# Attention, a dense MoE and a top-2 MoE in one kernel: the first expert's rows chosen in f32r, gate logits in 32-column tiles, bias rows of the start given to other engines, and named banks in the attention

## The chip, the cores and the metric

The kernel runs on one core of a Trainium2 chip. The time is the device time of one launch in microseconds (us); lower is better. A core has four compute engines with a queue each, which work in order: TensorE (PE; its weight loads are listed as PEld), VectorE (DVE), ScalarE (ACT) and GpSimd (POOL). SyncE (SP) issues most DMAs. Engines wait for one another by semaphores.

## The reference

Three stages follow one another, all in float32.

```python
scores = scale * q @ k.T                      # B=2, H=8, S=576, D=64
x = log1p(|i-j|) / log1p(max(i,1))
bias = relu(x * w1 + b1) @ w2                 # hidden 32, one bias per head
attn = softmax(scores + bias);  x = attn @ v  # -> 1152 tokens x 512
g = max(0.01*h, h), h = x @ w_in              # first MoE: 512 -> 2048 -> 512, dense
x = g @ w_out
noisy = x @ w_gate + log1p(exp(x @ w_noise)) * noise   # second MoE: 8 experts
top2, softmax over the two
out[mask] += weight * relu(x[mask] @ w1[e]) @ w2[e]    # 512 -> 1024 -> 512
```

## The kernel before, in words

**Attention.** Tokens go in nine blocks of 128 queries; a block has four pairs of heads, so there are 36 pairs. A pair's scores are made by TensorE (L1138), VectorE adds the bias and takes the row minimum (`add_bias`, L1149, tile `s`), ScalarE exponentiates (L1162), TensorE transposes the probabilities in three steps (`tp`, L1181 and L1183), each into a PSUM bank named `m` which ScalarE copies out (`tp_copy`, L1189, tile `pts`), and TensorE multiplies by V (`pv`, L1206). The banks named `m` are a pool of four under one name; the pool hands them out.

**The bias** is built in 36 groups of 16 queries; the first query block needs groups 0 to 7. A group is four `bias_relu` rows of 128x576 (on GpSimd for groups from `POOLED` = 5 on, L1034; otherwise three on VectorE, L1038, and one on ScalarE, L1036), eight matmuls with column tiles of 32 (`bias_mm`, L1048), a copy `bt` (ScalarE L1058 or L1060, VectorE L1062), and a store that rearranges it into the tile `bias` (L1069). Groups on GpSimd use a table of negated offsets. `add_bias` of the first pair needs the stores of groups 0 to 7.

**First MoE.** Weights and activations are split into a high and a low float32r part (`whi`, `wlo`, `xah`, `xal`), and each product is three float32r matmuls (L312 up, L342 to L344 down). Tokens go in two groups, five tiles of 128 and then four.

**Gate.** Each finished tile of 128 tokens is transposed (`gate_trans`, L363), copied out (`xt`, L370, L372) and multiplied by the 16 gate and noise columns (`gate_logits`, L380, four float32 matmuls with the 128 tokens as weights and 16 moving columns). A group's chain then follows: `gate_softplus` on ScalarE (tile `ez`, two functions with a table load each), `gate_top2` on VectorE, `gate_count` on TensorE (L431 to L434), `gate_slots`. Tiles are gated in the groups 0 to 2, 3 and 4, 5 and 6, 7 and 8.

**The passage.** Tokens are scattered by expert to `xs` in memory. For the first expert that is too late for tiles 5 to 8: their rows are chosen by a matmul with a 0/1 selection matrix (`sel` on VectorE, L517; `x_sel` on TensorE, L523, 128x320 in float32), and the rows of tiles 0 to 4 come back from memory and are added by matmuls with the identity (`x_early`, L528). The sums are split into `xah` and `xal` (L543, L545), and the first expert's `e_mm1` (also L312) and `e_mm2` (L584) follow.

**Order.** A planner of this kernel, `Plan`, is given every step with its engine, an estimated duration, the resources read and written, and a due time, and fixes the order of each engine's queue. Where a matmul in float32 is one row of the program, the trace shows two instructions.

Of the kernel before, what the change touches and what calls it, by code (L numbers as in the profile page):

```python
# [18 lines left out]
P = 128  # L19
# [11 lines left out]

BLOCKS = [(b, t) for t in range(4) for b in range(2)] + [(None, 4)]
# [9 lines left out]
POOLED = 5  # L42
# [89 lines left out]
class Moe:  # L132
# [15 lines left out]
    def steps(self, ident, zrow):  # L148
# [27 lines left out]
        def loads():  # L176
            self.wg = cp.tile([P, DC, 2 * E], F32, name="wg")
            nc.sync.dma_start(self.wg, self.t["wg"])
            self.nz = cp.tile([P, NT, E], F32, name="nz")
            nc.sync.dma_start(self.nz, self.t["nz"])  # L180
# [173 lines left out]

    def store_x2(self, t):
        for p0, m, t0 in token_runs(t):
            self.nc.sync.dma_start(self.x2d[t0:t0 + m, :], self.rows[t][p0:p0 + m, 0, :DM])
# [7 lines left out]
    def gate_copy(self, t, eng, c=slice(0, DM)):  # L365
        if ("xt", t) not in self.T:
            self.T["xt", t] = self.wk.tile([P, DC, P], F32, name="xt")
# [6 lines left out]
    def gate_logits(self, t, i, bank):  # L374
# [3 lines left out]
        lp = self.R["lp"][:, i * 2 * E:(i + 1) * 2 * E]  # L378
        for d in range(DC):
            self.nc.tensor.matmul(lp, xt[:, d, :], self.wg[:, d, :], start=(d == 0), stop=(d == DC - 1))  # L380

    def gate_softplus(self, nb, step):
        if step == 0:
            self.R["lg"] = lg = self.R["lp"][:, :nb * 2 * E].rearrange("p (i e) -> p i e", i=nb)
# [99 lines left out]
    def load_x(self, e, t):  # L484
        o, n = STILES[t]
        self.XR[e, t] = r = self.row()
        if e != "early":
            o, n = o + e * C1, P
# [8 lines left out]
    def load_early(self, q):  # L497
        self.load_x("early", q)
# [6 lines left out]
    def sel(self, t, i):  # L505
# [5 lines left out]
        self.T["sel", t] = s = self.T["sels"].pop(0).bitcast(F32)  # L511
# [126 lines left out]
    def run(self):  # L638
# [6 lines left out]
        def weight(n, key):  # L645
# [17 lines left out]
            wait = [("sel", NT - 3)] if n == U1 else [("x", 0, DC - 1)] if U1 < n < U1 + 8 else []  # L663
            add("ACT", .95, self.split, (n, 0), [f] + wait, [w], key - 4)
            add("DVE", 1.15, self.split, (n, 1), [f, w] + [("first", 0)] * (n == 1), [w], key - 4)
            return w

        def gates(ts, key):

            t0, nb = ts[0], len(ts)  # L670
            early = [("xe", q) for q in range(3)] if t0 >= GROUPS[1][0] else []
            for q, tt in enumerate(ts):
# [3 lines left out]
                xt = slot("xt", 2)  # L676
                new = [xt, ("xt1", xt[1])]
                add("PE", .43, self.gate_trans, (tt, 2 if late else 0), [row[tt, 0], row[tt, 3]], [b] + new, k)
# [3 lines left out]
                else:  # L682
                    add("ACT", .27, self.gate_copy, (tt, "ACT", half[0]), [b], new[:1], k)
                    add("DVE", .33, self.gate_copy, (tt, "DVE", half[1]), [b], new[1:], k)
                add("PE", .86, self.gate_logits, (tt, q, 1), new, [("tp", 1)], k + 45 * late)
# [16 lines left out]
            for q, tt in enumerate(ts):  # L702
                if tt >= GROUPS[1][0]:
                    first = tt == GROUPS[1][0]
                    if first:
                        sels[0] = slot("g", 5)
                    add("DVE", .3, self.sel, (tt, q), [("rec", 0), ("iota", 0)] + [sels[0]] * (not first),
                        [("sel", tt)] + [sels[0]] * first, k + 20 * (tt < NT - 2) - .2)
# [14 lines left out]

        def evac(i, tt, key):
# [9 lines left out]
            if tt < NT - 2:  # L734
                add("DVE", .6, self.evac_x2, (tt, i, 1, "DVE"), [(f"acc{i}", 0)] if tt < GROUPS[1][0] else [row[tt, 0], row[tt, 3]],
                    [row[tt, 1]], key + .2 + 60 * (tt >= b0 > 0))
# [19 lines left out]
        def up(g, f, k):  # L756
# [3 lines left out]
            xk = [("xb", d) for d in range(DC)] if g else []  # L760
# [13 lines left out]
        def x_sel(tt, d, key):  # L774
            add("PE", .54, self.x_sel, (tt, d), [("sel", tt), sels[0], row[tt, 0], row[tt, 3]], [(f"acc{d}", 0)], key)

        for g, (b0, nb, n) in enumerate(GROUPS):
            chunks = range(nb * P // n)
            tail = 4 if g else 0
            for f in range(nf1 - tail):  # L780
# [7 lines left out]
                if g == 0 and f in (10, 11, 12, 13):  # L788
                    d = f - 10
                    add("ACT", .53, self.split_x, (d, 0), [], [("xb", d)], t + 8)  # L790
                    add("DVE", .61, self.split_x, (d, 1), [("xb", d)], [("xb", d)], t + 8)
# [26 lines left out]
        for d in range(DC):  # L818
            for tt in (NT - 4, NT - 3):
                x_sel(tt, d, t + 10 + tt)  # L820

            add("PE", .27, self.x_early, (d,), [("xe", q) for q in range(3)] + [("tp", 0)], [(f"acc{d}", 0)], t + 20)
            for tt in (NT - 2, NT - 1):
                x_sel(tt, d, t + 30 + d + .1 * tt)
# [40 lines left out]
        for e in range(E):  # L865
            for f in range(nf2):
# [3 lines left out]
                h, gf = slot("h", 2), slot("g", 5)  # L870
                for part in [[d] for d in range(DC)] if e + f == 0 else [range(DC)]:
# [9 lines left out]
                if f == 0 and e == 0:  # L881
                    load(1, t)
                    add("DVE", .1, self.overflow_flag, (0,), [("rec", 0)], [("m", 0)], t)
                    b = ("tp", 0)
                    add("PE", .1, self.overflow_flag, (1,), [("m", 0)], [b], t)
                    add("DVE", .1, self.overflow_flag, (2,), [b], [], t)
# [85 lines left out]
class Attn:  # L972
    def __init__(self, ctx, tc, t, xa, xb, ident):
# [10 lines left out]
        self.ps_m = ctx.enter_context(tc.tile_pool(name="ps_m", bufs=4, space=bass.MemoryType.PSUM))  # L984
# [10 lines left out]
        nc.vector.tensor_scalar(self.scb[:, n:], self.scb[:, n:], small[:, 1:2], -1.0, op0=OP.mult, op1=OP.mult)  # L995
# [471 lines left out]
```

## Time and profile before

| | us |
|---|---|
| time, median of 3 runs (lowest to highest) | 685.68 (684.35 to 686.38) |
| time of the profiled execution | 689.21 |
| its span | 687.5 |
| TensorE busy in it | 654.7 |

The span runs from the first to the last recorded instruction; the profiled execution lasted 1.7 us longer than its span and 3.5 us longer than the median. Rows of the trace are given below, ahead of the prediction. In a timeline row the first number is the start, the second the length of the merged stretch, `x3` the number of instructions, and the bracket the idle time ahead of it and what ended it.

### The profile page before, as it was taken

Reading aid. Unit: us, or ns where it says so; the run is one execution under the profiler, and the core shown is the slowest. Engines: PE = TensorE matmul, PEld = TensorE weight load, DVE = VectorE, ACT = ScalarE, POOL = GpSimd, SP = SyncE. Lnnn points to the kernel's source line nnn. Section 1 sums busy time; section 2 is a strip of 40 time slices with the busy share of each in tenths; the row PEclk is TensorE's granted clock in tenths of the full one; section 3 lists DMA queues with packets and bytes.
Section 4 is the critical chain, followed back from the end, with each engine's and each line's share of the span. In section 5 each row is a group of like instructions: output and inputs, shape, how many; then the busy total and the mean of one; then the engine's idle time right before and its main releaser. Section 6 shows DMA issues by size and latency. Waiting matters only on the chain.

```text
span 687.5 us, 14783 instructions
## 1 busy us (share of the span) xinstructions
PE 654.7 (95%) x5777; PEld 553.0 (80%) x5777; DVE 458.0 (67%) x1010; ACT 342.9 (50%) x657; POOL 180.9 (26%) x215
## 2 busy tenths in 40 slices
PE   6799999999999998999999999999999999999992
PEld 2467766777789987999988997898888889888881
DVE  7589887976879878946656435565656465565621
ACT  5367766676674333445545345544434444444420
POOL 6867655541000000000042003103133140403311
PEclk9889999999999999999999999999999999999997
DMA  3785862326356787735245404658585776858521
GB/s 115 200 231 167 272 208 69 91 54 212 110 185 184 224 242 240 247 89 184 77 155 157 128 31 139 214 185 257 173 247 172 239 215 198 273 174 270 167 66 40
DMA packets 41629, 118.60 MB, mean 173 GB/s; under 512 B 6100, under 2 KB 6356, under 8 KB 39506
## 3 DMA queue, kind: packets, MB, share of 16 engines
q1 hardware_dynamic: 36850, 105.47, 49.8%
q0 software_dynamic: 4560, 11.71, 5.1%
q8 instruction: 47, 0.77, 0.5%
q10 hardware_dynamic: 144, 0.41, 0.2%
q14 instruction: 28, 0.23, 0.1%
HBM read 77.91 MB, written 30.75 MB: 158 GB/s over the span
## 4 chain that ended last, share of the span: by engine, by line
PE 79%; DVE 9%; DMA 5%; ACT 3%; issue 2%; POOL 0%; DVEq 0%; ACTq 0%; POOLq 0%
PE h L312 28%; PE acc L584 17%; PE m L1206 5%; PE sc L1138 5%; PE m L1181 4%; PE m L1048 4%; PE acc L344 4%; PE acc L342 3%; PE acc L343 3%; DMA wr<-in_w_in 3%; ACT pts L1189 2%; PE acc L523 1%; DMA wr<-in_w_out 1%; PE acc L380 1%; PE sc L1048 1%
## 5 line engine op out<-in xcount | busy, mean ns | idle before, releaser
L286 DVE TENSOR_TENSOR wlo<-wr,whi 128x1024 fp32r<-128x1024 f32 x96 | 117.1, 1222 | 55.9 <-ACT whi L283 51.4
L312 PE MATMUL h<-xah,whi 128*128 128x320 f32 x384 | 120.5, 314 | 0.3 <-DVE gg L329 0.3
L283 ACT ACTIVATE whi<-wr 128x1024 fp32r<-128x1024 f32 x96 | 101.2, 1056 | 36.4 <-PE acc L584 13.3
L312 PE MATMUL h<-xal,whi 128*128 128x320 f32 x384 | 119.1, 310 | 0.1
L312 PE MATMUL h<-xah,wlo 128*128 128x320 f32 x384 | 118.6, 309 | 0.0
L1034 POOL TENSOR_SCALAR up<-wl,small 128x576 f32<-128x576 f32 x124 | 96.9, 798 | 55.8 <-PE m L1048 46.0
L584 PE MATMUL acc<-whi,g 128*128 128x512 f32 x320 | 106.7, 398 | 0.0
L618 POOL DMA_INDIRECT out<-row x24 | 35.4, 1475 | 178.9 <-DVE row L609 140.2
L312 PEld LDWEIGHTS h<-xah,whi 128*128 128x128 f32 x384 | 72.4, 189 | 7.9 <-DVE gg L329 1.4
L558 ACT ACTIVATE g<-h 128x320 fp32r<-128x320 f32 x64 | 28.0, 437 | 98.8 <-PE h L312 43.9
L473 POOL DMA_INDIRECT xs<-rows,sidx x18 | 20.2, 1120 | 213.0 <-ACT lk L326 145.0
L312 PEld LDWEIGHTS h<-xal,whi 128*128 128x128 f32 x384 | 72.4, 189 | 4.5 <-DVE xal L545 0.9
L584 PE MATMUL acc<-wlo,g 128*128 128x512 f32 (+1 forms) x192 | 75.7, 395 | 0.0
L312 PEld LDWEIGHTS h<-xah,wlo 128*128 128x128 f32 x384 | 72.3, 188 | 0.0
L565 DVE SCALAR_TENSOR_TENSOR g<-h,g 128x64 fp32r<-128x64 f32 (+1 forms) x128 | 35.4, 318 | 51.9 <-ACT g L558 50.9
L1189 ACT ACTIVATE pts<-m 128x384 f32<-128x384 f32 (+1 forms) x108 | 50.0, 523 | 38.7 <-PE m L1181 35.2
L584 PEld LDWEIGHTS acc<-whi,g 128*128 128x128 f32 x320 | 56.9, 188 | 8.7
L344 PE MATMUL acc<-whi,g 128*128 128x512 f32 x144 | 56.8, 394 | 2.4 <-DVE g L333 2.4
L342 PE MATMUL acc<-whi,g 128*128 128x512 f32 x144 | 57.5, 399 | 0.0
L1162 ACT ACTIVATE pp<-s,mn 128x576 f32<-128x576 f32 x72 | 54.9, 767 | 5.1 <-DVE mn L1149 5.1
L343 PE MATMUL acc<-wlo,g 128*128 128x512 f32 x144 | 57.1, 396 | 0.0
L1149 DVE CUSTOM_DVE_ANT_0 s<-sc,bias 128x576 f32<-128x576 f32 x72 | 51.4, 747 | 1.1 <-PE sc L1138 1.1
(160 smaller groups left out, 1212.4 us busy)
## 6 DMA issues: line engine op xcount, KB each, us to landing
wr<-in_w SPq DMA_DIRECT2D x64, 512.0 KB
bias<-bt SPq DMA_DIRECT2D x40, 288.0 KB
wr<-in_w_in SPq DMA_DIRECT2D x8, 1024.0 KB
wr<-in_w_out SPq DMA_DIRECT2D x8, 1024.0 KB
wf<-wr SPq DMA_DIRECT2D x16, 512.0 KB
wr<-wf SPq DMA_DIRECT2D x16, 512.0 KB
row<-xs SPq DMA_DIRECT2D x23, 258.0 KB
xs<-xb SPq DMA_DIRECT2D x4, 1290.0 KB
```

The lines of the kernel that those rows point to most:

```text
L283: self.nc.scalar.activation(w[0], r, AF.Copy)
L286: self.nc.vector.tensor_tensor(out=lo, in0=r, in1=hi.bitcast(F32), op=OP.subtract)
L312: self.nc.tensor.matmul(h, u[:, d, :], v[:, d, :], start=(d == 0 and i == 0), stop=(d == DC - 1 and i == 2))
L342: nc.tensor.matmul(acc, gh, whi, start=(f == 0), stop=False)
L343: nc.tensor.matmul(acc, gh, wlo, start=False, stop=False)
L344: nc.tensor.matmul(acc, gl, whi, start=False, stop=(f == self.FF1 // P - 1))
L565: self.nc.vector.scalar_tensor_tensor(gl, h[:, c], 0.0, g[:, c].bitcast(F32), op0=OP.max, op1=OP.subtract)
L584: nc.tensor.matmul(y, u, v, start=(f == 0 and i == 0), stop=(last and i == len(prods) - 1))
L1034: self.nc.gpsimd.tensor_scalar(u, w, 3.0e38, b, op0=OP.min, op1=OP.max)
L1149: self.nc.vector.tensor_tensor_reduce(out=s.rearrange("p (a b) -> p a b", a=2), in0=sc[:, :, :288], in1=bias[:, h, :].rearrange("p (a b) - ...
L1162: self.nc.scalar.activation(p[:, a * SEQ:(a + 1) * SEQ], s, AF.Exp, bias=mn[:, 0:1], scale=-1.0, accum_out=sm[:, 0, a:a + 1])
L1189: self.nc.scalar.activation(ps, self.PT[blk, c, k][:, :n, :], AF.Copy)
```

## The change

It has four parts. **At the start** `POOLED` goes from 5 to 8: the 12 bias rows of groups 5, 6 and 7 leave GpSimd, nine for VectorE and three for ScalarE; the groups are built in the order 0 to 7; and the negated table with the part of `wl` that only GpSimd reads is prepared by a new step `negate` behind VectorE's last row, for which GpSimd's first row now waits. **In the attention** the four banks `m` get names of their own, `m0` to `m3`, and are used in turn. **At the gate** the logits of tiles 0 to 6 are made by `gate_quads`: the 16 gate columns, padded to 32, are the weights, a tile's 128 tokens are the moving columns, and each tile of a group has a column tile of 32 of its own; the result is copied and transposed back. Tiles 7 and 8 keep `gate_logits`. **In the passage** each of the rows of tiles 5 to 8 is split into a high and a low float32r part (`split_row`), `sel` is written as float32r, and `x_sel` is two float32r matmuls instead of one in float32. `x_early` always takes 128 rows. The copies of tiles 5 and 6, their `sel` and the overflow flag are held back to later places, the pieces of the first `e_mm1` come behind all of `x_sel`, and the first weight of the second MoE is split earlier.

```diff
-POOLED = 5
+POOLED = 8
+EARLY = [0, 128, C1 - 128]
...
+    def gate_quads(self, ts, bank):
+        xt = [self.T.pop(("xt", t)) for t in ts]
+        self.R["lq"] = lq = self.bank(bank)
+        for d in range(DC):
+            for i, x in enumerate(xt):
+                self.nc.tensor.matmul(lq[32 * i:32 * i + 32, :P], self.wg[:, d, :], x[:, d, :],
+                                      start=(d == 0), stop=(d == DC - 1))
+    def gate_quads_copy(self, nb):
+        self.nc.vector.tensor_copy(self.lt[:32 * nb, :], self.R["lq"][:32 * nb, :P])
+    def gate_quads_trans(self):
+        self.R["lp"] = lp = self.R["lq"][:, P:2 * P]
+        self.nc.tensor.transpose(lp, self.lt, self.ident)
...
+    def split_row(self, t, step):
+        hi, lo = self.row_parts(t)
+        r = self.rows[t][:, 0, :DM].rearrange("p (d c) -> p d c", d=DC)
+        if step == 0:
+            self.nc.scalar.activation(hi, r, AF.Copy)
+        else:
+            self.nc.vector.tensor_tensor(out=lo, in0=r, in1=hi.bitcast(F32), op=OP.subtract)
...
-        self.nc.tensor.matmul(self.T["x", 0, d][:, :C1], self.rows[t][:, 0, d * P:(d + 1) * P], self.T["sel", t],
-                              start=first, stop=(t == NT - 1))
+        for i, x in enumerate(self.row_parts(t)):
+            self.nc.tensor.matmul(self.T["x", 0, d][:, :C1], x[:, d, :], self.T["sel", t],
+                                  start=(first and i == 0), stop=(t == NT - 1 and i == 1))
...
-            self.nc.tensor.matmul(self.T["x", 0, d][:, o:o + n], self.XR["early", q][:n, d * P:(d + 1) * P],
-                                  self.ident[:n, :n], start=False, stop=False)
+            self.nc.tensor.matmul(self.T["x", 0, d][:, o:o + n], self.XR["early", q][:, d * P:(d + 1) * P],
+                                  self.ident[:, P - n:], start=False, stop=False)
...
-            wait = [("sel", NT - 3)] if n == U1 else [("x", 0, DC - 1)] if U1 < n < U1 + 8 else []
+            wait = [("we", 0)] if n == U1 + 1 else [("x", 0, DC - 1)] if U1 + 1 < n < U1 + 8 else []
...
+    def bank(self):
+        self.banks += 1
+        return self.ps_m.tile([P, 512], F32, name=f"m{self.banks % 4}")
...
+    def negate(self):
+        n = 4 * POOLED
+        self.nc.vector.tensor_scalar(self.scb[:, n:], self.scb[:, n:], self.small[:, 1:2], -1.0, op0=OP.mult, op1=OP.mult)
+        self.scale_wl(slice(WL1, WL1 + P))
...
-        for i, G in enumerate((0, 5, 1, 2, 6, 3, 4, 7)):
+        for i, G in enumerate(range(8)):
...
+        add("DVE", .5, self.negate, (), [("row6.2", 0)], [("neg", 0)], -2.2)
```

VectorE's queue at the start, before (`pp` and `u` are bias rows, `ql` and `kp` splits of Q and K, `bt` the copies of groups 8 and 9, the last row `add_bias`):

```order
L1006 TENSOR_SCALAR wl<-wl,small 128x807
L1038 TENSOR_SCALAR pp<-wl,small 128x576 x3
L1038 TENSOR_SCALAR u<-wl,small 128x576 x3
L1109 SCALAR_TENSOR_TENSOR ql<-raw,qh 128x512
L1038 TENSOR_SCALAR pp<-wl,small 128x576 x3
L1083 TENSOR_TENSOR kp_97<-raw,kp_97 128x576
L1038 TENSOR_SCALAR u<-wl,small 128x576 x3
L1038 TENSOR_SCALAR pp<-wl,small 128x576 x3
L1062 TENSOR_SCALAR bt<-m,small 128x288 x2
```

The same place of the change:

```order
L1117 TENSOR_SCALAR pp<-wl,small 128x576 x3
L1117 TENSOR_SCALAR u<-wl,small 128x576 x3
L1188 SCALAR_TENSOR_TENSOR ql<-raw,qh 128x512
L1117 TENSOR_SCALAR pp<-wl,small 128x576 x3
L1117 TENSOR_SCALAR u<-wl,small 128x576 x3
L1162 TENSOR_TENSOR kp_96<-raw,kp_96 128x576
L1117 TENSOR_SCALAR pp<-wl,small 128x576 x3
L1117 TENSOR_SCALAR u<-wl,small 128x576 x3
L1117 TENSOR_SCALAR pp<-wl,small 128x576 x3
L1117 TENSOR_SCALAR u<-wl,small 128x576 x3
L1088 TENSOR_SCALAR small<-small 128x112
L1079 TENSOR_SCALAR wl<-wl,small 128x128
```

VectorE has 24 bias rows there instead of 15, and the last two rows, `negate`, are what GpSimd's first row waits for.

TensorE's queue in the passage, before, behind the logits of tile 7 (`h` is the bank of tile 8's transposes, the four `acc` the four quarters of the model width):

```order
L363 MATMUL h<-ident,rows 128x128 x4
L523 MATMUL acc_6028<-g,rows 128x320
L523 MATMUL acc_6036<-g,rows 128x320
L380 MATMUL acc_6006<-wg,xt 128x16 x4
L523 MATMUL acc_6048<-g,rows 128x320
L523 MATMUL acc_6054<-g,rows 128x320
```

The same place of the change, from tile 8's transposes on:

```order
L380 MATMUL h<-ident,rows 128x128 x4
L397 MATMUL acc_6011<-wg,xt 128x16 x4
L557 MATMUL acc_6056<-g,xbh 128x320
L557 MATMUL acc_6056<-g,xbl 128x320
L557 MATMUL acc_6061<-g,xbh 128x320
L557 MATMUL acc_6061<-g,xbl 128x320
```

No `x_sel` stands between the transposes and the logits of tile 8 any more; 16 float32r rows of tiles 5 and 6 follow them, then half of `x_early`, the count (L464 to L467), and the rest.

Further on in the same queue, before, behind `x_early` (`xah` and `xal` are the first expert's input, `ofm` the overflow flag):

```order
L523 MATMUL acc_6028<-g,rows 128x320 x2
L633 MATMUL tp<-ident,ofm 1x128
L523 MATMUL acc_6036<-g,rows 128x320 x2
L312 MATMUL h<-xah,whi 128x320
L312 MATMUL h<-xal,whi 128x320
L312 MATMUL h<-xah,wlo 128x320
L523 MATMUL acc_6048<-g,rows 128x320
```

The same place of the change, the end of `x_sel` and the beginning of the first expert:

```order
L557 MATMUL acc_6070<-g,xbh 128x320
L557 MATMUL acc_6070<-g,xbl 128x320
L557 MATMUL acc_6070<-g,xbh 128x320
L557 MATMUL acc_6070<-g,xbl 128x320
L317 MATMUL h<-xah,whi 128x320
L317 MATMUL h<-xal,whi 128x320
L317 MATMUL h<-xah,wlo 128x320
```

The first expert's pieces no longer stand between the selections; the 16 float32r rows of tiles 7 and 8 are all ahead of them, and the flag is behind.

## Rows read from the trace of the kernel before

**Rows 1.** The page: span; busy time, share, instructions of each engine

```profile
span 687.5 us, 14783 instructions
PE 654.7 (95%) x5777; PEld 553.0 (80%) x5777; DVE 458.0 (67%) x1010; ACT 342.9 (50%) x657; POOL 180.9 (26%) x215
```

**Rows 2.** Windows: stretch, busy us (instructions), PEclk, DMA share, GB/s

```profile
404.00:438.00 34.00, 33.67 (x203) 27.47 (x203) 18.62 (x91) 18.38 (x36) 7.87 (x8) 1.00 0.33 110
438.00:660.00 222.00, 222.00 (x1267) 197.64 (x1266) 136.73 (x237) 100.69 (x156) 56.11 (x42) 1.00 0.70 217
...
29.18:31.50 2.32, 2.22 (x12) 1.71 (x12) 1.24 (x5) 1.51 (x4) 2.32 (x4) 0.50 0.82 209
```

**Rows 3.** Line L1038: ns least/median/most, first and last start

```profile
L1038 DVE TENSOR_SCALAR pp<-wl,small x9: 520/995/1002, 6.1 to 19.5; 128x576 f32<-128x576 f32 x9
```

**Rows 4.** Timeline of VectorE and GpSimd, 5 to 33 us: start, length

```profile
8.34 2.83 DVE L1038 TENSOR_SCALAR u<-wl,small 128x576 f32<-128x576 f32 x3
14.36 0.74 DVE L1083 TENSOR_TENSOR kp<-raw,kp 128x576 fp32r<-128x576 f32 x1
...
6.14 15.72 POOL L1034 TENSOR_SCALAR up<-wl,small 128x576 f32<-128x576 f32 x16 [4.76 <-DVE wl L1006]
22.44 2.90 POOL L1034 TENSOR_SCALAR up<-wl,small 128x576 f32<-128x576 f32 x4 [0.58 <-PE sc L1048]
```

**Rows 5.** Timeline of ScalarE at the start

```profile
6.42 0.76 ACT L1036 ACTIVATE pp<-wl,small 128x576 f32<-128x576 f32 x1
7.08 0.67 ACT L1081 ACTIVATE kp<-raw 128x576 fp32r<-128x576 f32 x1
13.33 0.74 ACT L1058 ACTIVATE bt<-sc,small 128x576 f32<-128x576 f32 x1
```

**Rows 6.** The chain that ended last, 20 to 29 us, in order of time

```profile
22.84 0.84 ACT bt L1060
23.70 3.65 DMA bias<-bt
28.36 0.66 DVE s L1149
```

**Rows 7.** Timeline of TensorE before the first transposes

```profile
29.18 1.50 PE L1138 MATMUL sc<-kp,qh 64*128 64x288 f32 x4 [2.32 <-DVE mn L1149]
31.56 1.75 PE L1181 MATMUL m<-ident,pp 128*128 128x128 f32 x7
```

**Rows 8.** Waits of TensorE, 95 to 115 us, and its timeline there

```profile
PE m L1181 <- ACT pts L1189: 2.6, 4, 0.6
...
101.09 0.55 PE L1181 MATMUL m<-ident,pp 128*128 128x128 f32 x3 [0.64 <-ACT pts L1189]
102.66 0.27 PE L1183 MATMUL m<-ident,inv 128*128 128x128 f32 x1
102.86 1.18 PE L1048 MATMUL m<-up,small 128*32 128x288 f32 x16
103.86 1.06 PE L1206 MATMUL m<-pts,vt 128*32 128x128 f32 x32
```

**Rows 9.** Timeline of TensorE at the gate of the first tiles

```profile
333.50 0.96 PE L380 MATMUL acc<-wg,xt 128*128 128x16 f32 x8
```

**Rows 10.** Timeline of TensorE in the passage

```profile
420.91 3.48 PE L523 MATMUL acc<-g,rows 128*128 128x320 f32 x12
424.49 4.06 PE L528 MATMUL acc<-ident,row 128*128 128x128 f32 x24
437.30 0.31 PE L312 MATMUL h<-xah,wlo 128*128 128x320 f32 x1
437.45 0.63 PE L584 MATMUL acc<-whi,g 128*128 128x512 f32 x2
```

**Rows 11.** Timeline of ScalarE and VectorE at the last tiles' gate

```profile
421.09 0.18 ACT L386 ACTIVATE ez<-acc 128x16 f32<-128x16 f32 x1 [1.16 <-issue]
...
425.93 0.68 DVE L517 TENSOR_SCALAR g<-iota_c,y 128x320 f32<-128x320 f32 x2
```

More of the change, by code (lines that the diff above doesn't have):

```diff
@@ L683, in gates @@
                     add("ACT", .27, self.gate_copy, (tt, "ACT", half[0]), [b], new[:1], k)
-                    add("DVE", .33, self.gate_copy, (tt, "DVE", half[1]), [b], new[1:], k)
-                add("PE", .86, self.gate_logits, (tt, q, 1), new, [("tp", 1)], k + 45 * late)
+                    add("DVE", .33, self.gate_copy, (tt, "DVE", half[1]), [b], new[1:] + [("turned", 0)], k)
+                if late:
+                    add("PE", .86, self.gate_logits, (tt, q, 1), new, [("tp", 1)], k + 45)
+            if not late:
+                add("PE", .6, self.gate_quads, (ts, 1), sum(xts, []), [("tp", 1)], k)
+                add("DVE", .25, self.gate_quads_copy, (nb,), [("tp", 1)], [("lt", 0)], k)
+                add("PE", .2, self.gate_quads_trans, (), [("lt", 0)], [("tp", 1)], k)
+            for x in later:
+                x(key + 60, [("turned" if late else "lt", 0)])
+            later.clear()
+            if late:
+                for q, tt in enumerate((NT - 4, NT - 3)):
+                    add_sel(tt, q, key + 50, [("turned", 0)])
             k = key + .5
@@ L701, in gates @@
             add("DVE", 1.6, self.gate_slots, (t0, nb), [R, ("ef", 0), ("we", 0), ("tp", 0)], [("rec", 0)], k)
[L702 to L708, printed above, removed]
+            if late:
+                for q, tt in enumerate(ts):
+                    add_sel(tt, q, k - .2, [])
             for q, tt in enumerate(ts):
@@ L722, in gates, with copies @@
                 add("DVE", .08 * nb, self.gate_run, (nb,), [R], [("run", 0)], k + .3)
+        def copies(i, tt, key, wait):
+            r, x = [row[tt, 0], row[tt, 3]], [(f"xb{d}.{i // 2}", 0) for d in range(DC)]
+            add("ACT", .53, self.split_row, (tt, 0), r + wait, x + [("rh", tt)], key + .1)
+            add("DVE", .6, self.split_row, (tt, 1), r + [("rh", tt)] + wait, [("rl", tt)], key + .1)
+            if tt < NT - 2:
+                add("DVE", .6, self.evac_x2, (tt, i, 1, "DVE"), r + wait, [row[tt, 1]], key)
         def evac(i, tt, key):
@@ L774, in x_sel @@
         def x_sel(tt, d, key):
-            add("PE", .54, self.x_sel, (tt, d), [("sel", tt), sels[0], row[tt, 0], row[tt, 3]], [(f"acc{d}", 0)], key)
+            add("PE", .29, self.x_sel, (tt, d), [("sel", tt), sels[0], ("rh", tt), ("rl", tt)], [(f"acc{d}", 0)], key)
         for g, (b0, nb, n) in enumerate(GROUPS):
@@ L819, in run @@
             for tt in (NT - 4, NT - 3):
-                x_sel(tt, d, t + 10 + tt)
-            add("PE", .27, self.x_early, (d,), [("xe", q) for q in range(3)] + [("tp", 0)], [(f"acc{d}", 0)], t + 20)
+                x_sel(tt, d, t + 6 + .1 * tt)
+            add("PE", .6, self.x_early, (d,), [("xe", q) for q in range(3)], [(f"acc{d}", 0)], t + 7.5)
             for tt in (NT - 2, NT - 1):
-                x_sel(tt, d, t + 30 + d + .1 * tt)
+                x_sel(tt, d, t + 7 + .3 * d + .1 * tt)
         xsall = [("xs", tt, x) for tt in range(NT) for x in range(2)]
@@ L1044, in bias_mm @@
         else:
-            bp = self.ps_m.tile([P, 512], F32, name="m")[:, None, :]
+            bp = self.bank()[:, None, :]
         for k, n in enumerate(halves):
@@ L1177, in tp @@
         p = self.PP[blk, c][0]
-        pt = self.ps_m.tile([P, 512], F32, name="m").rearrange("p (a b) -> p a b", a=4)
+        pt = self.bank().rearrange("p (a b) -> p a b", a=4)
         for j in range(3):
@@ L1195, in pv @@
         pts = [self.PT.pop((blk, c, k)) for k in range(3)]
-        xt = self.ps_m.tile([P, 512], F32, name="m")[:, :P]
+        xt = self.bank()[:, :P]
         self.X[blk, c] = xt, pts[2][:, 3, :]
```

76 lines of the change are left out of this document (49 added, 27 removed).

## Prediction, made before the changed kernel ran

> **What bounds the kernel now.** The page comes first. TensorE is busy for 654.7 of 687.5 us [rows 1], so some 33 us are idle at most, and a saving is either TensorE work in a stretch where it never stops or one of its waits. The windows say which stretch is which. From 438 to 660 us TensorE is busy for 222.0 of 222 us at full clock, with DMA at 0.70, and in the passage from 404 to 438 us for 33.67 of 34 [rows 2]. An instruction taken from TensorE there moves all that follows. The start is of the other kind: the chain that ended last runs from 22.84 through a ScalarE copy, a store (3.65 us) and VectorE to the first `add_bias` at 28.36 [rows 6], and TensorE waits 2.32 us for it before 29.18 [rows 7]. Last, the list of TensorE's waits has one family between 95 and 115 us: four waits of transposes for ScalarE's copies, 2.6 us in all [rows 8].
>
> I make the sum against the profiled execution, 689.21 us, and take it from the median of the runs, 685.68, since the two differ by 3.5 us on the same program. For this kernel 0.3% (2.1 us) is about what a measurement can tell from no change.
>
> **A. The start.** VectorE's bias row has a median of 995 ns and a least of 520 [rows 3]. The short one is the first, at 6.1 us, and GpSimd begins its 16 rows at 6.14 [rows 4]; every later row ran beside GpSimd. GpSimd shows the same from its side: 16 rows took 15.72 us (0.98 each) beside VectorE, and the four at 22.44, when VectorE stood idle, 2.90 (0.73) [rows 4]. Instructions of a queue overlap by some 0.07 us (three rows in 2.83, not 2.99 [rows 4]), so a row costs 0.92 beside GpSimd and 0.45 without it. The change keeps GpSimd idle until VectorE's last row. VectorE then has 24 x 0.45 = 10.8 us, two splits of about 0.7 (one is shown) [rows 4] and little waiting: from 6.0 to about 18.5. ScalarE is nearly as full: eight rows and eight copies of 0.76 and 0.74 less the overlap, and three splits of 0.6 [rows 5], 8 x 0.69 + 8 x 0.67 + 1.8 = 12.7 us from 5.9, to 18.6 if it never waited. Its last copy needs VectorE's last row and a last pair of matmul groups (about 0.9 us), then 0.74: about 20.2, where it now ends at 23.68 [rows 6]. The store's 3.65 us then land at 23.9. Group 8's copies stand ahead of the first `add_bias` in VectorE's queue, and they are timed by GpSimd: `negate` by 19.0, four GpSimd rows (2.90) by 21.9, matmuls and two copies of about 1 us each by 23.9. Both meet at about 24.1 where 28.36 stands now: **-4.3 us**. Queued behind are the K and V loads on SP, whose queue is freed as much earlier. Bounds: if VectorE rows cost half-way between, 0.58, 24 of them add 3.1 us, -1.2; if the crowding that follows pair 0 shrinks too, -6. I take -4.3, since the 520 ns row is the very operation.
>
> **B. The banks.** Four times a transpose step waits 0.64 us for the copy of the step just before it [rows 8]: the pool gave the bank used last, although three others were older. With names in turn a step's bank is four uses old, and its copy long done: 4 x 0.64 = 2.56 us, TensorE being without other idle time there. **-2.4**, between 0 (the wait passes to the next pair) and -2.6.
>
> **C. The gate of tiles 0 to 4.** One tile's logits take 0.96 us as eight instructions, 0.80 start to start [rows 9], each dominated by loading 128 weights for 16 columns. The change has 4 x 3 matmuls for a group of three tiles, in column tiles of 32. Attention has the same form: 32 instructions of 128 moving columns in column tiles took 1.06 us [rows 8], 0.033 each, so four run side by side and one alone costs about four times that, 0.11 to 0.13. A group thus costs 8 x 0.11 = 0.86 to 1.0 us however many tiles share it, and a transpose of 0.1. Five tiles go from 4.0 to about 1.9: **-2.1**. If the column tiles did not overlap, 40 instructions of 0.11 are 4.4, +0.4 and the transposes.
>
> One rule speaks against it. Attention steps from full width to column tiles between 102.66 and 102.86 [rows 8], 0.20 us with no wait listed, about 0.1 more than a transpose's own pace. The Trainium skill (TensorEngine Tiling (Array Packing), Key Properties) says that changing the tiling mode drains TensorE. By the trace's list of waits nothing is lost there, and C is -2.1; by the rule, with 0.1 us at each of two changes per group as its size, C is -1.7 and the median 672.0.
>
> **D. The passage.** The 32 `x_sel` instructions (16 matmuls) run at 3.48/12 = 0.29 us [rows 10]; 32 float32r ones of the same 320 columns at the pace of the first expert's, 437.45 - 437.30 = 0.15 [rows 10]. All of it on TensorE: -4.5 us. What counts is when each half can start.
> - *Up to tile 8's logits.* They end at about 420.9, where the next row starts [rows 10]. Four `x_sel` instructions (1.2 us) leave the place ahead of them, the gate of tiles 5 and 6 costs 0.6 less as in C, and as that cover is gone TensorE waits some 0.6 for tile 8's copy: 419.7.
> - *Tile 7 and 8's chain.* From `ez` at 421.09 to the last selection at 425.93 + 0.68 = 426.6 are 5.5 us [rows 11], with two table loads, on ScalarE and VectorE. It moves with the logits: 419.8 to 425.3; the held-back copies and four row splits now stand in the same two queues (each about 0.55 to 0.65 by the splits in [rows 4, 5]), and I give them 0.4: 425.7. TensorE has 16 x 0.15 + 24 `x_early` instructions meanwhile, which cost 4.06 now (0.17 each) and 2.9 if at the 0.12 of [rows 9], which also load 128 weights: it comes to the late rows between 425.2 and 426.4. I take 426.1; before it was 424.49 + 4.06 = 428.5 [rows 10]: -2.4.
> - *From there to `e_mm2`.* Now 437.45 - 428.5 = 8.9 us: 16 x 0.29 + 24 x 0.15 = 8.2 of work, 0.7 of waiting for splits. After: 16 x 0.15 + 24 x 0.15 = 6.0 at least; the splits of the first quarter run beside the selections of the others. -2.9, or -2.4 if the waits stay.
>
> Together **-5.3**, the gate of tiles 5 and 6 in it; bounds -3 (below) and -6.9 (TensorE never waits). Behind it the weights of the second MoE must keep up: from 438 on DMA is at 0.70 and TensorE waited for none [rows 2], and the loads start with the same steps.
>
> **Sum.** -4.3 - 2.4 - 2.1 - 5.3 = -14.1: the profile 675.1, the median **671.6 us**.
>
> **The rivals.**
> 1. *The passage's gain becomes a wait.* The late chain is no shorter, and the held-back steps lengthen it by up to 2 us (two splits and a copy ahead of it on each engine); TensorE stands for 2.3 us more, and, as after the 2.32 us before 29.18, when the granted clock was 0.50, half of 2.4 GHz, from 29.18 to 31.5 [rows 2, 7], the next few us run at half pace. D gives -5.3 + 2.3 = -3.0, or 0 with 3 us lost to the clock: 674 to 677. For it: the chain of 5.5 us against 5.2 to 6.7 us of cover. Against: TensorE was never idle there, and selections can overtake the copies.
> 2. *VectorE's rows stay at 0.92.* Then 24 rows last 22.1 us, and `add_bias` comes at 24.1 + 24 x 0.47 = 35.4, 7 us later than now: -9.8 + 7.0, 683. The 520 ns row speaks against it; that it is a single one, for it.
> 3. *Slower: the named banks make every pair wait.* A bank is now taken by turn, not by age of release; where the bank of `pv` or of a bias group is still unread at its turn, a pair waits. The price of one is 0.64 [rows 8]; 36 pairs make 23 us, and 685.7 - 11.7 + 23 = 697. It decides from (4.3 + 2.1 + 5.3)/36 = 0.33 us a pair. Against it: the order of use equals the order of release in the pairs without a wait.
> 4. *The column tiles don't overlap*, so the gate's change does nothing: C is +0.4 for -2.1, and D's share 0.6 less: 675.
>
> **How the numbers follow.** The forecast, with its terms within their bounds, has 0.66 (667 to 675 alone); the first rival 0.18; the second 0.06; the third 0.03; the fourth 0.07. The range reaches from all terms at their far bounds but one, 667, to the first rival with the clock and a start of half size, 679.5. Faster by over 0.3% are the forecast, the first, the fourth and a third of the second: 0.93. The rest of the second is the same, 0.03, or with the third slower, 0.04.
>
> **What would show it.** A: VectorE's bias rows near 0.52 us, the first `add_bias` near 24, the first transposes near 27 where 31.56 stands [rows 7]. B: no transpose waits for `pts` around 100. C: the gate's matmuls under 1.1 us per group. D: `x_sel` at 0.15 each, the late half from 426 less what came before, about 417, and the same 6 us from there to `e_mm2`; from there on TensorE full. The prediction is wrong where VectorE's rows stay near 1 us, where a wait for selections or splits longer than 2 us stands in the passage with a clock of 0.5 behind it, or where transposes wait for banks in most pairs.

## The result, and the profile after

The changed kernel takes 675.75 us (median of 4 runs, 673.21 to 676.53), the kernel before beside it 686.03: ratio 0.9848, 95% interval 0.9816 to 0.9880. Run once more with 6 runs it took 672.91, ratio 0.9821 (0.9782 to 0.9860). It is faster by 10 to 12 us; 14.1 were forecast, and the time lies inside the range.

The page's first lines, as in [rows 1]:

```profile
span 673.7 us, 14803 instructions
PE 640.5 (95%) x5780; PEld 544.2 (81%) x5780; DVE 455.9 (68%) x1027; ACT 344.9 (51%) x664; POOL 170.4 (25%) x205
```

TensorE is busy for 14.2 us less and waits as much as before; in a second pair of profiles (before_again and after_again below) it is 11.1 us less. By stage (the windows, columns as in [rows 2]):

```profile
29.00:55.00 26.00, 24.00 (x410) 17.53 (x404) 23.24 (x61) 20.33 (x46) 19.32 (x31) 1.00 0.87 239
404.00:438.00 34.00, 32.31 (x209) 28.96 (x208) 22.54 (x94) 20.28 (x33) 8.32 (x8) 1.00 0.56 180
438.00:660.00 222.00, 221.54 (x1258) 196.22 (x1256) 131.14 (x233) 95.30 (x151) 56.23 (x42) 1.00 0.64 202
```

The granted clock from 29 to 55 us is 1.00, 2.4 GHz. In the profile before, it fell to 0.50, 1.2 GHz, from 29.18 [rows 2]; the mean there from 29 to 36 us is 0.51. The passage has 1.7 us of idle TensorE where it had 0.3.

To see where the time went I read four moments from TensorE's timeline in each profile: the first matmul of the first MoE (`h<-xah`: the attention is over), the first of its second token group (`h<-xbh`), the first `e_mm2`, and the end of the span. The runs are introduced below.

| kernel | attention over | first MoE, first group | from there to `e_mm2` | span |
|---|---|---|---|---|
| before | 199.16 | 113.27 | 125.02 | 687.5 |
| before_again | 197.51 | 109.56 | 125.03 | 682.4 |
| changed | 190.14 | 114.46 | 117.95 | 673.7 |
| after_again | 189.33 | 111.40 | 117.86 | 669.3 |
| undo_start | 191.74 | 113.88 | 117.19 | 673.9 |
| undo_banks | 193.25 | 112.02 | 117.20 | 674.3 |
| undo_start_banks | 197.71 | 111.20 | 117.83 | 677.5 |
| no_hold | 192.33 | 112.18 | 117.22 | 672.8 |
| early_loads | 191.42 | 113.03 | 117.21 | 672.3 |
| early_v | 194.04 | 110.49 | 117.20 | 672.3 |
| undo_gate | 189.00 | 114.36 | 121.67 | 676.5 |
| sel_f32 | 189.06 | 115.28 | 122.78 | 677.3 |
| delay_9 | 200.27 | 111.18 | 118.73 | 680.8 |
| delay_18 | 208.72 | 113.23 | 117.83 | 691.6 |

The attention and the passage repeat from profile to profile; the first MoE scatters over more than 5 us. That is why no single pair of profiles gives the change's worth: the first two differ by 13.8 us in the span, before_again and the changed kernel by 8.7. One of before_again's ten executions took 2019.32 us; it is not the profiled one and stands in no ratio here.

**The start.** The timelines that answer to [rows 4 to 7] (start, length; the bracket is the idle time ahead and what ended it):

```profile
16.46 1.37 DVE L1117 TENSOR_SCALAR u<-wl,small 128x576 f32<-128x576 f32 x3
17.94 0.28 DVE L1079 TENSOR_SCALAR wl<-wl,small 128x128 f32<-128x128 f32 x1
...
18.32 14.77 POOL L1113 TENSOR_SCALAR up<-wl,small 128x576 f32<-128x576 f32 x19 [16.94 <-DMA raw<-in_kd]
...
19.65 0.68 ACT L1160 ACTIVATE kp<-raw 128x576 fp32r<-128x576 f32 x1 [0.64 <-DMA raw<-in_kd]
20.24 0.72 ACT L1137 ACTIVATE bt<-sc,small 128x576 f32<-128x576 f32 x1
...
24.69 0.76 DVE L1228 CUSTOM_DVE_ANT_0 s<-sc,bias 128x576 f32<-128x576 f32 x1 [0.79 <-DMA bias<-bt]
...
27.23 1.20 PE L1260 MATMUL m<-ident,pp 128*128 128x128 f32 x9
31.89 0.42 PE L1285 MATMUL m<-pts,v 128*32 128x128 f32 x8 [0.94 <-DMA v<-in_v]
```

VectorE's last three bias rows begin at 16.46 and take 1.37 us instead of 2.83; GpSimd begins behind `negate`; ScalarE's last copy runs from 20.24 to 20.96, where its end was forecast for 20.2: VectorE's last row is done at 17.83, but the split of a K load stands ahead of the copy in ScalarE's queue, and ScalarE waits 0.64 us for that load. The first `add_bias` is at 24.69, held by the store (forecast 24.1; before 28.28); in after_again it is at 25.30. Pair 0's transposes begin at 27.23 instead of 31.56, and its product with V then waits 0.94 us for a V load. All 12 rows of one tile take the same time (ns least/median/most):

```profile
L1117 DVE TENSOR_SCALAR u<-wl,small x12: 511/512/514, 6.8 to 17.3; 128x576 f32<-128x576 f32 x12
```

**The banks.** Two pairs near 90 us, nine transposes in one stretch each and no wait, where [rows 8] has stretches of three:

```profile
89.97 1.20 PE L1260 MATMUL m<-ident,pp 128*128 128x128 f32 x9
94.41 1.21 PE L1260 MATMUL m<-ident,pp 128*128 128x128 f32 x9
```

**Gate and passage.** TensorE's timeline: the gate of tiles 5 and 6 (L405 and the transpose back, L413), the logits of tile 8, the early selections, `x_early` in two halves, the late selections, `e_mm2`:

```profile
399.46 1.07 PE L405 MATMUL acc<-xt,wg 128*32 128x128 f32 x16
401.27 0.27 PE L413 MATMUL acc<-ident,lt 128*128 128x128 f32 x1
...
408.88 1.12 PE L397 MATMUL acc<-wg,xt 128*128 128x16 f32 x8 [0.47 <-ACT xt L387]
410.05 0.41 PE L557 MATMUL acc<-g,xbh 128*128 128x320 f32 x1
...
412.49 1.45 PE L562 MATMUL acc<-ident,row 128*128 128x128 f32 x12
...
413.90 1.53 PE L562 MATMUL acc<-ident,row 128*128 128x128 f32 x12
416.61 0.38 PE L557 MATMUL acc<-g,xbh 128*128 128x320 f32 x1 [1.17 <-DVE g L550]
...
418.88 0.31 PE L557 MATMUL acc<-g,xbl 128*128 128x320 f32 x1
...
422.55 0.63 PE L618 MATMUL acc<-whi,g 128*128 128x512 f32 x2
```

Two tiles' logits take 1.07 us as 16 instructions; the three of the first group took the same 1.07 us as 24, from 326.74. The early selections run at 0.15 us, `x_early` takes 1.45 + 1.53 us for 4.06, TensorE waits 1.17 us for the late selections, and from 416.61 to `e_mm2` are 5.9 us, where 8.9 were.

### The profile page after: what moved, and what is told of

Read it like the earlier page. It is cut to its first block, busy times and chain, and to the rows that moved or that the text cites. A ratio compares the mean times of both kernels' runs of the same rounds, so it can differ in the third digit from the quotient of the medians.

```text
span 673.7 us, 14803 instructions
## 1 busy us (share of the span) xinstructions
PE 640.5 (95%) x5780; PEld 544.2 (81%) x5780; DVE 455.9 (68%) x1027; ACT 344.9 (51%) x664; POOL 170.4 (25%) x205
## 4 chain that ended last, share of the span: by engine, by line
PE 77%; DVE 8%; DMA 8%; ACT 3%; issue 2%; SPq 0%; POOL 0%; DVEq 0%; ACTq 0%; POOLq 0%
PE h L317 27%; PE acc L618 18%; PE m L1285 5%; PE sc L1217 5%; DMA wr<-in_w_in 4%; PE m L1260 4%; PE acc L347 3%; PE acc L348 3%; PE acc L349 3%; PE m L1127 3%; DMA raw<-in_kd 2%; ACT pts L1268 2%; DMA wr<-in_w_out 1%; DVE wlo L291 1%; PE sc L1127 1%
## 5 line engine op out<-in xcount | busy, mean ns | idle before, releaser
L288 ACT ACTIVATE whi<-wr 128x1024 fp32r<-128x1024 f32 x96 | 101.4, 1056 | 49.3 <-DVE wr L276 13.8
L1113 POOL TENSOR_SCALAR up<-wl,small 128x576 f32<-128x576 f32 x112 | 84.8, 777 | 58.6 <-PE m L1127 37.8
```

The lines of the kernel that those rows point to most:

```text
L288: self.nc.scalar.activation(w[0], r, AF.Copy)
L1113: self.nc.gpsimd.tensor_scalar(u, w, 3.0e38, b, op0=OP.min, op1=OP.max)
```

## The experiments

Each ratio is to the kernel before, beside which it ran; an interval is about 0.002 to 0.004 wide to either side, 1.4 to 3 us. "Changed" below means the kernel after, of which 674 us is a fair middle (675.75 and 672.91).

**before_again** is the kernel before, unedited.

> The kernel before, unchanged, for a second profile and for the spread of its runs. The first profile (689.21 us) lay 3.2 us above the median of 686.03. Theory: the difference is the granted clock, which was 0.50 in 29.2 to 34 us and 46 to 48 us; a second profile then comes at 684 to 687 us with less of its start at half clock, and the ratio is 1.000 within 0.003. Rival: the half clock belongs to this kernel's start in each run (TensorE waits 2.3 us ahead of it); then the second profile shows it at the same places, with a span of 686 to 688 us.

Measured: ratio 0.9996 (0.9971 to 1.0022), profile 684.15 us. Its window:

```profile
30.00:35.00 5.00, 5.00 (x35) 3.48 (x36) 2.58 (x8) 2.68 (x7) 1.71 (x3) 0.50 0.97 331
```

The half clock stands in the same place, so it belongs to this kernel's start in the executions seen; the second dip of the first profile, at 46 to 48 us, is gone. The span is 5.1 us shorter, 3.7 of it in the first MoE. Both theories were half right, and the first profile lay at the long end of its kernel's executions.

**undo_start** gives the start its old form.

```diff
-POOLED = 8
+POOLED = 5
-        for i, G in enumerate(range(8)):
+        for i, G in enumerate((0, 5, 1, 2, 6, 3, 4, 7)):
-        add("DVE", .5, self.negate, (), [("row6.2", 0)], [("neg", 0)], -2.2)
```

> The changed kernel with the start as before (12 bias rows back on GpSimd, old order of groups, negated table at once); the other three parts kept. Theory of the prediction: the start alone is worth 4.3 us, so 680 us, ratio to before 0.991; VectorE's bias rows at 0.92 us beside GpSimd again, first add_bias near 28.3. Rival: the start's gain in the profile (29.2 to 24.7 for the first add_bias) is mostly given back in the attention or the first MoE; then 676 to 677 us, ratio 0.986.

Measured: 675.36 us, ratio 0.9848 (0.9816 to 0.9881). The first `add_bias` is back at 27.75, 2.4 to 3.1 us later than in the changed kernel's two profiles, the attention ends 1.6 to 2.4 us later, and the time is 1.4 us over the middle, within the noise. The rival's number is nearer. TensorE waits the same 2.3 us ahead of the first pair as in the kernel before, but the clock here stayed full:

```profile
27.75 0.74 DVE L1229 CUSTOM_DVE_ANT_0 s<-sc,bias 128x576 f32<-128x576 f32 x1
...
30.00:35.00 5.00, 4.08 (x73) 2.82 (x72) 3.90 (x11) 3.67 (x11) 3.93 (x6) 1.00 0.97 338
```

**undo_banks** puts the four banks under one name again.

```diff
-        return self.ps_m.tile([P, 512], F32, name=f"m{self.banks % 4}")
+        return self.ps_m.tile([P, 512], F32, name="m")   # pool of bufs=4
```

> The changed kernel with one pool of four banks under one name; the order of every engine stays the same. Theory of the prediction: four waits of 0.64 us come back near 100 us and the time is 2.4 us longer: 678.2 us, ratio to before 0.9885. Rival: the waits depended on the start's timing and don't come back: 675.8 us, ratio 0.985. Third: names in turn cost other pairs something, and this one is faster than 675 us.

Measured: 678.15 us, ratio 0.9885 (0.9850 to 0.9919); the attention ends 3.1 to 3.9 us later. The prediction's theory holds, with a larger size. The waits are the old ones; here in undo_start_banks, which has them too:

```profile
98.41 0.55 PE L1261 MATMUL m<-ident,pp 128*128 128x128 f32 x3
99.60 0.55 PE L1261 MATMUL m<-ident,pp 128*128 128x128 f32 x3 [0.64 <-ACT pts L1269]
100.78 0.55 PE L1261 MATMUL m<-ident,pp 128*128 128x128 f32 x3 [0.64 <-ACT pts L1269]
```

**no_hold** makes the negated table at once, so that GpSimd starts beside VectorE.

```diff
+        nc.vector.tensor_scalar(self.scb[:, n:], self.scb[:, n:], small[:, 1:2], -1.0, op0=OP.mult, op1=OP.mult)
+        self.scale_wl(slice(WL1, TABS[0][1]))
-        add("DVE", .5, self.negate, (), [("row6.2", 0)], [("neg", 0)], -2.2)
```

> The changed kernel, but the negated table is made at once, so GpSimd makes its first eight rows (groups 8 and 9) beside VectorE's rows from about 5 us on, instead of behind the last of them. Theory: beside GpSimd a VectorE row costs 0.92 us instead of 0.45; eight GpSimd rows last about 7.8 us, in which VectorE makes 8.5 rows instead of 17, so VectorE's last row ends some 3.9 us later (22 for 18), the first add_bias comes near 28 instead of 24.7, and the time is 3 to 4 us longer: 679 us, ratio 0.990. Rival: the rows' slowness was not GpSimd's doing; then VectorE's rows stay at 0.52 us, the first add_bias comes at 24 to 25, and the time stays at 675.8 us or falls.

Measured: VectorE's rows of one tile (ns), GpSimd's eight, and the first `add_bias`:

```profile
L1118 DVE TENSOR_SCALAR u<-wl,small x12: 505/512/996, 7.7 to 20.8; 128x576 f32<-128x576 f32 x12
...
5.53 7.99 POOL L1114 TENSOR_SCALAR up<-wl,small 128x576 f32<-128x576 f32 x8 [4.14 <-DVE wl L1080]
...
27.89 0.76 DVE L1229 CUSTOM_DVE_ANT_0 s<-sc,bias 128x576 f32<-128x576 f32 x1
```

Rows are 512 ns in the median and 996 at most, and the first `add_bias` comes at 27.89, as the theory had it (28): beside GpSimd a VectorE row takes twice as long. But the time is 674.49 us, ratio 0.9828 (0.9798 to 0.9857), no longer than the changed kernel's, where 3 to 4 us more were expected; the attention ends 2.2 to 3.0 us later.

**after_again** is the changed kernel once more.

> The changed kernel once more, for the spread. Five profiles so far spent 109.6 to 114.5 us between the first and the last part of the first MoE (first xah to first xbh matmul), the changed kernel the most, 114.5. Theory 1: that length varies from execution to execution with the landing of weight loads; then this profile has another length, 110 to 113 us, with other waits for gg and g. Theory 2: the earlier end of the attention is given back there in every execution; then it is 114 to 115 us again, with the two waits of about 2 us at the same places. Time 674 to 677 us by both, ratio 0.985.

Measured: 672.91 us; the first MoE took 111.40 us and had one wait of each kind:

```profile
PE h L317 <- DVE gg L334: 1.1, 1, 1.1
PE acc L349 <- DVE g L338: 1.2, 1, 1.2
```

Theory 1: the length varies with the execution. The clock has a part in it: in before, undo_start, sel_f32 and delay_18, four of the six longest, it fell to 0.50 for 2 to 4 us within the first MoE (0.50 from 268 to 270 us in before). In the changed kernel's first profile VectorE stood for weights and TensorE behind it (VectorE's first pass over a weight, then TensorE):

```profile
250.42 0.69 DVE L272 TENSOR_SCALAR wr<-wr 128x1024 uint32<-128x1024 uint32 x1 [2.11 <-DMA wr<-in_w_out]
270.55 0.69 DVE L272 TENSOR_SCALAR wr<-wr 128x1024 uint32<-128x1024 uint32 x1 [3.22 <-DMA wr<-in_w_in]
...
252.70 0.42 PE L317 MATMUL h<-xah,whi 128*128 128x320 f32 x1 [1.70 <-DVE gg L334]
272.84 0.42 PE L317 MATMUL h<-xah,whi 128*128 128x320 f32 x1 [2.15 <-DVE gg L334]
```

**undo_start_banks** has only gate and passage changed.

> The changed kernel with the start and the banks as before: only gate and passage changed. If the four terms add as the prediction has them (start 4.3, banks 2.4), it takes 675.75 + 6.7 = 682.5 us, ratio 0.995. If gate and passage are worth what the profiles show from the first xbh matmul on (7.1 to 7.8 us less to the first e_mm2, 0.8 to 1.1 more behind it), it takes 679 to 680 us, ratio 0.990, and start and banks together only 3.5 to 4. In the profile the attention ends as in the kernel before (197.5 us), or 1.8 us sooner where the granted clock is full from 30 to 35 us.

Measured: 679.51 us, ratio 0.9912 (0.9882 to 0.9942), as the second reading had it. Gate and passage are worth about 6 us, start and banks together about 5.5. The clock is low here too, 0.66 on average from 30 to 35 us.

**undo_gate** uses the old logits for tiles 0 to 6.

```diff
+                add("PE", .86, self.gate_logits, (tt, q, 1), new, [("tp", 1), ("lt", 0)], k + 45 * late)
-                add("PE", .6, self.gate_quads, (ts, 1), sum(xts, []), [("tp", 1)], k)
-                add("DVE", .25, self.gate_quads_copy, (nb,), [("tp", 1)], [("lt", 0)], k)
-                add("PE", .2, self.gate_quads_trans, (), [("lt", 0)], [("tp", 1)], k)
```

> The changed kernel with the old logits for tiles 0 to 6 (one tile after the other, 16 moving columns). Theory: column tiles overlap, so the old form costs 2.1 us more for tiles 0 to 4 and 0.6 for tiles 5 and 6, of which a part is cover in the passage: 678 to 678.5 us, ratio 0.988; from the first xbh matmul to e_mm2 about 119.5 to 120 us instead of 117.2 to 118. Rival: switching to column tiles and the extra transpose cost what is saved: 675.8 us and 117.5 us.

Measured: 676.42 us, ratio 0.9871 (0.9828 to 0.9913), 2.4 us over the changed kernel's middle. From the first `xbh` matmul to `e_mm2` the profile shows 121.67 us, 3.8 more, of which I estimate about 1.7 for a dip of the clock that the changed kernel's two profiles don't have (0.95, 0.50 and 0.69 in three stretches of 2 us: 0.1 + 1.0 + 0.6):

```profile
412.00:414.00 2.00, 2.00 (x9) 2.00 (x9) 1.36 (x4) 1.95 (x4) 1.69 (x2) 0.50 0.77 299
```

What is left, 2.1, is a little under the forecast 2.7.

**sel_f32** makes the selections in float32 and keeps the rest.

```diff
-        for i, x in enumerate(self.row_parts(t)):
-            self.nc.tensor.matmul(self.T["x", 0, d][:, :C1], x[:, d, :], self.T["sel", t],
-                                  start=(first and i == 0), stop=(t == NT - 1 and i == 1))
+        self.nc.tensor.matmul(self.T["x", 0, d][:, :C1], self.rows[t][:, 0, d * P:(d + 1) * P],
+                              self.T["sel", t].bitcast(F32), start=first, stop=(t == NT - 1))
```

> The changed kernel with the selection matmuls in float32 (16 of them, two instructions each, 0.29 us an instruction); row splits and all orders are kept. Theory: the late half, behind the selections, is 16 x 0.145 = 2.3 us longer and shows in full; of the early half's 2.3 us the wait for the late selections (1.17 us in the profile) absorbs half: 3.4 us in all, 679.2 us, ratio 0.990; TensorE's wait for the selection is gone. Rival: the early half hides wholly behind the late chain: 2.3 us, 678 us.

Measured: 675.27 us, ratio 0.9851 (0.9812 to 0.9889), less than the 679.2 expected, whose 0.990 lies just outside the interval, and not to be told from the changed kernel by time alone. The profiled execution, 679.09 us, was the longest of six. In it the step to `e_mm2` is 4.9 us longer, an estimated 1.7 of it by a dip of the clock from 410 to 414 us (0.52 and 0.63: 1.0 + 0.7), so 3.2 for the 3.4 of the theory; the median of the six doesn't confirm it. The late selections:

```profile
419.19 4.57 PE L556 MATMUL acc<-g,rows 128*128 128x320 f32 x16 [0.34 <-DVE g L550]
```

They take 4.57 us for 2.58 (416.61 to 419.19), and the wait ahead of them fell to 0.34.

**early_loads** releases K and V loads by the store of group 4 (`landed = [("st", 4)]` for 7).

> The changed kernel with the K and V loads released after the store of group 4 instead of group 7, which puts the third K load and the first V loads ahead of group 8's store in SP's queue. In the changed kernel TensorE waits 0.94 us for V in pair 0, and the ramp from pair 0 to pair 4 takes 20.9 us where four steady pairs take 17.8, with DMA at 0.95 to 1.05 from 25 to 45 us. Theory: the start's gain is lost because these loads are issued only at 24.5 us; issued some 3 us sooner, they shorten the ramp by 1 to 2 us: attention ends at 188 us, time 672 to 673, ratio 0.981. Rival: DMA is full in this stretch whatever the order, the early loads delay the stores and the first add_bias by as much; time and end of attention as in the changed kernel (189.3 to 190.1 us; 673 to 675.8).

Measured: 675.42 us, ratio 0.9845 (0.9812 to 0.9878), the attention over at 191.42, 1.3 to 2.1 us later than in the changed kernel. The theory fails: the wait for V is gone, but TensorE now waits 1.74 us for an `add_bias` that stands behind the split of a later K load, and the granted clock dips. The rival has the time and the full DMA engines right; it did not have the later end.

```profile
32.95 0.70 PE L1217 MATMUL sc<-kp,qh 64*128 64x288 f32 x3 [1.74 <-DVE mn L1228]
...
25.00:35.00 10.00, 7.95 (x102) 5.70 (x94) 8.33 (x22) 5.88 (x13) 9.27 (x12) 0.91 1.02 223
```

**early_v** releases the first batch's V loads by the stores of groups 0 to 3.

> The changed kernel with the V loads of the first batch released by the stores of groups 0 to 3, one after the other: the first V load goes out near 13 us, the others ahead of the last K loads. Theory of late loads: the 0.94 us wait for V in pair 0 vanishes and the ramp gets 1 to 2 us shorter, attention ends near 188.5 us, ratio 0.981. Rival: the second K load, now behind the V load, lands later than 19.6 us and with it ScalarE's last copy of the bias (which stands behind the K split in its queue), so the first add_bias comes about 0.5 to 1 us later and nothing is gained.

Measured: 674.39 us, ratio 0.9826 (0.9792 to 0.9860). The second K load now lands behind V, and ScalarE's last copy, queued behind that K's split, comes at 24.68 instead of 20.24; TensorE waits for it (us in all, times, longest):

```profile
PE sc L1217 <- ACT bt L1137: 4.9, 1, 4.9
```

The first `add_bias` comes at 29.78, and the attention ends 3.9 to 4.7 us late, at 194.04: the rival's mechanism at five times its size. The time hardly shows it. The profiled execution's first MoE was short, 110.49 us, but 674.39 is the median of six, and why the loss doesn't show in it stays open.

**delay_9** and **delay_18** put 18 and 36 passes more ahead of the first bias row, to see whether the first MoE gives a gain back.

```diff
         self.scale_wl(slice(WL1 + P, TABS[0][1]))
+        for _ in range(18):   # 36
+            nc.vector.tensor_scalar(self.wl[:, WL1 + P:], self.wl[:, WL1 + P:], 1.0, None, op0=OP.mult)
```

> The changed kernel with 18 more VectorE passes over the offset table (times 1.0, in place, about 0.5 to 0.6 us each) ahead of the first bias row, so that everything from there on comes 9 to 11 us later and nothing else changes. Ten profiles so far show a shorter first MoE the later the attention ends (113.5 us where it ends at 189 to 190, 110 to 111 where it ends at 197 to 199). Theory 1: the first MoE gives back a part, about a third, of what the attention gains, whatever the gain's source; then a delay of 9 to 11 us costs 6 to 7.5, 680 to 681.5 us, ratio 0.991 to 0.993, and the first MoE takes 110 to 111 us. Theory 2: its length only scatters with the landing of weight loads; then the delay costs all of 9 to 11 us, 683 to 685 us, ratio 0.996 to 0.998, and the first MoE takes 111 to 114.5.

> The same with 36 passes, a delay of 18 to 22 us. Theory 1: a third comes back, or all that the first MoE can give (3 to 4 us): 687 to 690 us, ratio 1.002 to 1.006. Theory 2: the whole delay shows: 692 to 696 us, ratio 1.009 to 1.015.

Measured: 685.94 us, ratio 1.0011 (0.9990 to 1.0032), and 693.30, ratio 1.0120 (1.0099 to 1.0141). The passes of delay_18:

```profile
5.24 19.70 DVE L1067 TENSOR_SCALAR wl<-wl 128x679 f32<-128x679 f32 x36
```

19.7 us more at the start made 693.3 - 674 = 19 us more in all, and 9.8 made 12, a little over theory 2's 683 to 685. Theory 2: of delays of this size nothing is given back. The apparent trend of shorter first MoEs behind later attentions is no evidence against it: delay_18, the attention over at 208.72, has 113.23 us, though with a dip of the clock in it.

## Why the prediction was right, and by how much it was off

**A, the start: the mechanism right, the worth too large.** VectorE's row took 0.43 us start to start for 0.45, and no_hold shows that GpSimd's presence is what makes the rows slow. Two things made "-4.3" too large. First, the forecast let the last copy wait for VectorE's last row and its matmuls; these were done, and the K split held the copy, which ended 0.8 us late. The first `add_bias` came at 24.69 and 25.30 for 24.1. Second, the start of 28.36 from which it was counted was a late one: with the old start it came at 27.64 to 27.75 in before_again, undo_start and undo_start_banks. So the first `add_bias` gained 2.3 to 3.6 us, not 4.3. Behind it nothing need be lost: against undo_start, after_again is 2.45 us sooner at the first `add_bias` and 2.41 at the end of the attention. The changed kernel's first profile is 3.1 and 1.6 us sooner; there 0.94 us goes to a V load, and 1.1 to a stop in pair 11 for which the trace names no cause:

```profile
83.92 0.49 PE L1285 MATMUL m<-pts,vt 128*32 128x128 f32 x9 [1.10 <-issue]
```

It stands in a stretch in which DMA is full; after_again doesn't have it, and before_again, undo_banks and delay_9 lose 0.8 to 1.1 us in the same pair. By time alone A is not shown: undo_start is 1.4 us over the changed kernel's middle and no_hold 0.5, both within the noise.

**Not in the sum: the clock at the start.** In the two pairs of profiles the attention ends 9.0 and 8.2 us sooner, and A and B explain 5 to 6 of it. Both profiles of the kernel before run at half clock from 29 to about 36 us, neither profile of the changed kernel does. Up to the end of the attention before_again and undo_start differ by the banks and by this, and by 5.8 us; with 3.1 to 3.9 for the banks, the half clock is worth 2 to 2.7 us, as an estimate from these differences. No run shows that the new start keeps the clock up: undo_start has the old start and 1.00. For the same reason undo_banks against undo_start_banks, 4.5 us at the end of the attention, is not A alone.

**B, the banks: right mechanism, too small.** Forecast -2.4, measured -3.1 to -3.9 at the end of the attention and -4 in time (undo_banks; undo_start_banks against undo_start has the same in time, but another clock). The term was four listed waits of 0.64. From a pair's last transpose to the next pair's, a pair with waits lasts 6.15 to 6.19 us instead of 4.44 (undo_banks and the changed kernel), so two pairs lose 3.5. The list counts only from the modelled end of the last transpose; three pipelined ones go on in 0.35 us but end after 0.55.

**C and D, gate and passage: right.** Forecast -7.4 together, measured -7.1 to -7.2 at `e_mm2`. TensorE waited where D said: 0.47 us for tile 8's copy (forecast 0.6), 1.17 for the late selections. D had at most 0.5 there, its chain of 6.0 us from tile 8's logits against 5.5 of cover; the chain took 6.56 (410.05 to 416.61). In undo_start, undo_banks, no_hold, early_loads and early_v, whose passage is the same, this wait was 0.4 us and the gain 7.8. `x_early` came out near its lower bound, 2.98 us for 2.9 to 4.1, and 4.06 before. The first rival's long stall did not come in the changed kernel; its low clock did in undo_gate, sel_f32 and delay_9, for 2 to 4 us in the passage.

**Not in the sum: the second MoE, +0.6 to +1.0.** Between the first and the last `e_mm2` the changed kernel's two profiles have 237.0 and 236.7 us, those of the kernel before 236.0. The overflow flag now stands behind `e_mm2` (0.12), and the second expert's first transposes wait:

```profile
443.95 0.55 PE L568 MATMUL tp<-ident,row 128*128 128x128 f32 x3 [0.38 <-DVE xal L579]
```

**The sum.** -2 - 3.5 - 7.1 + 0.8 is -11.8, without a term for the clock, and the two ratios give 10.4 and 12.3 us. The forecast of 14.1 was 2 to 4 us too large, most of it in A. That it equals the difference of the first two profiles, 13.8, is chance: the scatter of the first MoE (109.6 to 115.3 us) lies between them, and the two profiles of either kernel, paired in all ways, differ by 8.7 to 18.2. Two of the prediction's bounds don't come out of its own numbers: a row half-way between 0.45 and 0.92 costs 0.69 us, not 0.58, and 24 of them would have put A at about +1.3 instead of -1.2; and all four terms at their far bounds (6, 2.6, 2.1 and 6.9) give 668, not 667.

The second and third rivals (bias rows at 0.92, a bank wait in each pair) did not come, as the bias rows of 511 to 514 ns and the rows of the banks above show; nor did the fourth, by the 1.07 us for two tiles and for three and by undo_gate. The prediction's rule that changing the tiling mode drains TensorE, from the Trainium skill (TensorEngine Tiling (Array Packing), Key Properties), could not be told apart: two tiles' logits and the transpose back came to 1.07 us and one transpose, with no wait listed, where C had 0.86 to 1.0 and 0.1.

## What to carry to other kernels

Move element-wise work between engines only after looking at what it costs while its neighbour runs: here the same row took 0.51 or 1.0 us. Look, too, at what stands in the queue ahead of the last step of the path: here a K split held it. Cost a repeated wait by the distance between equal instructions of two neighbouring repetitions, not by the idle time listed. Before a difference between two profiles is read as the worth of a change, a second profile of each kernel shows which stages repeat and which scatter.

## What the runs showed of the hardware that was not expected

VectorE's rows beside GpSimd took 996 ns for 512, and GpSimd's 0.98 us for 0.73. Start to start the two together make 1/0.92 + 1/0.98 = 2.1 rows in a us, VectorE alone 1/0.43 = 2.3 (three in 1.29): the second engine brings less than nothing. The Trainium skill (GPSIMD Engine Reference, the table of specifications) says that GpSimd shares its SBUF interfaces with VectorE, with contention where VectorE's instruction is in a 2-port perf mode or has two SBUF inputs. The two rates agree with a shared interface; no run here shows which mode these rows ran in. The granted clock fell to 0.50, 1.2 GHz, in the passage of undo_gate, sel_f32 and delay_9 for 2 to 4 us, behind 0.47 us of listed idle ahead of tile 8's logits or transposes. delay_9's passage is the changed kernel's own, with the same 0.47 us, and in both profiles of the changed kernel the clock stayed at 1.00; why it falls in one execution and not in another stays open. At the start it is the same: behind a wait of 2.3 us it fell in both profiles of the kernel before and in undo_start_banks, and not in undo_start.
